# Causal attention and a channel mixer on one core: the values product in 64x64 tiles, the first queries loaded as they lie, and 16-bit copies that GpSimd may take

## The chip, the cores and the metric

The kernel runs on one core of a Trainium2 chip. TensorE (PE) multiplies, VectorE (DVE), ScalarE (ACT) and GpSimd (POOL) do the rest, SyncE (SP) issues most transfers. The metric is the device time of one execution in microseconds, as the median of several runs.

## The reference

```python
scores = scale * q @ k.T            # q, k, v: 4 batches x 12 heads x 448 x 64, float32
scores = where(upper triangle, -1e9, scores)
attn = exp(scores - max) / (sum + 1e-9)
x = attn @ v                        # heads side by side: 4 x 448 x 768
h = relu(x.T @ w_tok1) @ w_tok2     # 448 -> 256 -> 448, over tokens
u = x + h.T
out = u + relu(u @ w_ch1) @ w_ch2   # 768 -> 1536 -> 768, over channels
```

The six mixer products and the weights are handled as sums of a rounded part and its remainder, three products for one; attention runs in float32, in which PE executes each product as two instructions.

## The kernel before

Two heads of one batch form a pair, 24 pairs in all. For each pair `load_pair` loads k, q and v, `prep` turns k and q so that the 64 channels lie along partitions, `heads` makes scores, exponentials and sums, `by_tensor` (pairs 0 to 9, transposes on PE) or `by_dma` (pairs 10 to 23, a DMA transpose of 16-bit halves: a `split` before it, a `merge` behind it) turns the probabilities into the tile `pt`, and `values` multiplies them with v and copies the sums from PSUM into `u`. Every third pair is followed by `xturn` and `tokens`, each batch by `split_u`; the channel products of batches that are done (`product` and its callers) fill PE between the pairs and are alone on it from about 300 us on.

No engine's order is written out. `plan.job` records each step with its engine and costs, and `Plan.emit` hands out the steps: on a free engine the one of lowest rank whose needs are met. The rank is a number from the table PLACES, and where a step may run on more than one engine the table CHOICE says which (a, d, p, s for ACT, DVE, POOL, SP). The order is fixed when the program is built; each engine works through its list and waits at semaphores. Where the plan finds PE without work before 75 us, it puts in a product whose result is not used (`keep_warm`, L865).

PE takes its array as one 128x128 tile, two tiles of 128x64, two of 64x128 or four of 64x64. A values product before is eight (pairs 0 to 9) or four pieces per head in 128x64 tiles (L1245), then eight products for the keys and queries that are left, the tips, in 64x64 tiles (L1254). Scores (L1021) are in 64x64, transposes of probabilities and of x (L1115, L1291) in 64x128, channel and token products (L1433, L1350, L1383) in 128x128, and the first pairs' k and q are turned by 112x64 tiles (L916).

A transfer reports to one of eight semaphores (DMAHW0 to DMAHW7), which the program gives out in turn over all queues. The issue of the ninth transfer therefore waits until the first has landed, and so on.

Of the kernel before, what the change touches and what calls it, by code (L numbers as in the profile page):

```python
# [21 lines left out]
    "load_pair.blocks": {-2: (0, 1), 10: (129, 153), 12: (193, 224), 14: (242, 259), 16: (338, 293), 18: (405, 420),  # L22
        20: (522, 537), 22: (578, 591), 24: (670, 694), 26: (742, 758), 28: (831, 851), 30: (911, 927), 32: (996,
        1006), 34: (1056, 1070), 36: (1141, 1151), 38: (1205, 1220), 40: (1280, 1293), 42: (1333, 1348), 44: (1406,
        1426)},
    "load_pair.load": {0.5: (2,), 2.5: (3,), 4.5: (178,), 6.5: (209,), 8.5: (274,), 10.5: (312,), 12.5: (393,),
        14.5: (453,), 16.5: (490,), 18.5: (558,), 20.5: (615,), 22.5: (704,), 24.5: (773,), 26.5: (822,), 28.5:
        (902,), 30.5: (949,), 32.5: (1047,), 34.5: (1114,), 36.5: (1194,), 38.5: (1241,), 40.5: (1376,), 42.5:
        (1441,), 44.5: (1489,), 46.5: (1531,)},
    "load_pair.upper": {-0.2: (12,), 1.8: (15,), 3.8: (213,), 5.8: (245,), 7.8: (317,), 9.8: (380,), 11.8: (441,),  # L30
        13.8: (505,), 15.8: (519,), 17.8: (592,), 19.8: (651,), 21.8: (727,), 23.8: (821,), 25.8: (859,), 27.8:
        (938,), 29.8: (982,), 31.8: (1077,), 33.8: (1136,), 35.8: (1226,), 37.8: (1269,), 39.8: (1401,), 41.8:
        (1462,), 43.8: (1517,), 45.8: (1561,)},
    "narrow.load": {3.5: (6, 9, 16, 62, 86, 121, 114, 144), 12: (288,), 13: (371,), 14: (445,), 15: (503,), 16:
        (606,), 17: (665,), 18: (755,), 19: (818,), 20: (897,), 21: (974,), 22: (1041,), 23: (1120,), 24: (1191,),
        25: (1254,), 26: (1328,), 27: (1400,), 28: (1463,), 29: (1511,), 30: (1553,), 31: (1599,), 32: (1627,), 33:
        (1660,), 34: (1687,), 35: (1730,)},
    "narrow.size": {3.5: (32, 52, 61, 116, 133, 177, 180, 235), 12: (352,), 13: (413,), 14: (484,), 15: (545,), 16:
        (642,), 17: (705,), 18: (786,), 19: (854,), 20: (932,), 21: (1013,), 22: (1072,), 23: (1153,), 24: (1223,),
        25: (1291,), 26: (1360,), 27: (1437,), 28: (1497,), 29: (1532,), 30: (1584,), 31: (1616,), 32: (1646,), 33:  # L40
        (1676,), 34: (1712,), 35: (1748,)},
    "narrow.shift": {3.5: (37, 56, 73, 125, 142, 183, 186, 263), 12: (359,), 13: (424,), 14: (491,), 15: (554,), 16:
        (646,), 17: (710,), 18: (793,), 19: (863,), 20: (939,), 21: (1019,), 22: (1084,), 23: (1157,), 24: (1227,),
        25: (1295,), 26: (1371,), 27: (1446,), 28: (1503,), 29: (1538,), 30: (1588,), 31: (1621,), 32: (1649,), 33:
        (1678,), 34: (1720,), 35: (1750,)},
# [6 lines left out]
    "prep.turn": {-1.5: (5, 8), 10.5: (199, 216), 12.5: (253, 271), 14.5: (286, 304), 16.5: (375, 384), 18.5: (449,
        486), 20.5: (562, 577), 22.5: (609, 626), 24.5: (702, 734), 26.5: (767, 790), 28.5: (877, 895), 30.5: (943,
        995), 32.5: (1014, 1034), 34.5: (1087, 1140), 36.5: (1166, 1176), 38.5: (1229, 1239), 40.5: (1304, 1315),
        42.5: (1368, 1378), 44.5: (1440, 1456)},
    "heads.<lambda>": {0: (11, 13), 2: (51, 57), 4: (94, 101), 6: (141, 160), 8: (197, 233), 10: (251, 267), 12:
# [1921 lines left out]
```

## Time and profile before

| | |
|---|---|
| time, median of 3 runs | 537.71 us (537.52 to 538.35) |
| the profiled execution's own time | 538.04 us |
| its span in the profile | 536.2 us |
| PE busy | 529.8 us |
| DVE, ACT, POOL busy | 426.4, 314.0, 164.2 us |
| granted TensorE clock | 1.0 in the mean |

Busy time is the time in which at least one instruction of the engine runs. A row of the timeline has the start, the time from the first start to the last end, the engine, the line, the operation, the tile written and those read, shape and count; in brackets stands how long the engine had been idle and what ended that. In rows of PE the tile shape stands ahead of the moving data's, as in 64*64 64x448.

### The profile page before, as it was taken

The numbers are of one execution on the slowest core, as the hardware profiler recorded it, in microseconds if no ns is written. First come the engines' busy times: TensorE is split into PE (matmuls) and PEld (weight loads), VectorE is DVE, ScalarE is ACT, GpSimd is POOL, SyncE is SP. The second block draws the span as 40 slices with busy tenths as digits, with TensorE's granted clock in tenths as the row PEclk, the third lists the DMA queues.
The fourth block names the chain that finished last, engine by engine and source line by source line (L and its number), as shares of the span: only waits on it lengthen the run. The fifth ranks groups of instructions, "written<-read, shape, count | busy, mean of one in ns | idle before, by whom it ended". The sixth has DMA issues, their size and how long they took to land.

```text
span 536.2 us, 12037 instructions
## 1 busy us (share of the span) xinstructions
PE 529.8 (99%) x4391; PEld 460.6 (86%) x4391; DVE 426.4 (80%) x1030; ACT 314.0 (59%) x768; POOL 164.2 (31%) x220
## 2 busy tenths in 40 slices
PE   8999999999999999999999999999999999999997
PEld 4778888888888888888898899999999999999996
DVE  5998899989797999888896679677877848485665
ACT  4998898899888787789784561243232313131300
POOL 2565745444252232332452132140010012321200
PEclk9999999999999999999999999999999999999999
DMA  9966677979999998999969327648213030212147
GB/s 194 198 116 144 152 214 160 215 153 233 207 178 200 225 190 193 205 196 229 210 163 198 115 92 205 131 119 162 88 32 116 7 91 23 87 32 88 31 75 131
DMA packets 221546, 77.72 MB, mean 145 GB/s; under 512 B 195760, under 2 KB 210992, under 8 KB 221488
## 3 DMA queue, kind: packets, MB, share of 16 engines
q1 hardware_dynamic: 207984, 74.90, 63.1%
q10 hardware_dynamic: 13504, 2.07, 2.1%
q8 instruction: 34, 0.56, 0.5%
q14 instruction: 24, 0.20, 0.2%
HBM read 49.15 MB, written 14.94 MB: 120 GB/s over the span
## 4 chain that ended last, share of the span: by engine, by line
PE 94%; SPq 2%; DVE 2%; ACT 1%; DMA 1%; issue 0%; POOL 0%; DVEq 0%; POOLq 0%
PE ps L1433 33%; PE ps L1860 16%; PE ps L1765 12%; PE ps L1021 6%; PE ps L1245 6%; PE ps L1383 6%; PE ps L1350 6%; PE ps L1836 3%; PE ps L1254 1%; PE ps L1115 1%; PE ps L1291 1%; SPq L940 1%; PE ps L865 1%; ACT prob L1055 1%; DMA gh<-in_k_dram 1%; PE ps L910 0%
## 5 line engine op out<-in xcount | busy, mean ns | idle before, releaser
L1500 DVE TENSOR_TENSOR u<-ps,u 128x448 f32<-128x448 f32 x118 | 72.5, 619 | 34.2 <-PE ps L1860 28.0
L1055 ACT ACTIVATE prob<-prob,stat 128x192 f32<-128x192 f32 (+6 forms) x168 | 83.7, 501 | 14.4 <-DVE stat L1043 14.1
L643 POOL TENSOR_TENSOR wl<-wf,wh 128x768 fp32r<-128x768 f32 x26 | 49.5, 1904 | 94.4 <-ACT wh L632 59.4
L1043 DVE CUSTOM_DVE_ANT_0 prob<-ps,mask 128x128 f32<-128x128 f32 (+6 forms) x168 | 63.3, 415 | 7.3 <-PE ps L1021 6.9
L634 POOL TENSOR_SCALAR prob<-prob,stat 128x64 f32<-128x64 f32 (+6 forms) x80 | 43.8, 559 | 55.4 <-DVE stat L1077 42.9
L1433 PE MATMUL ps<-uh,wh 128*128 128x448 f32 x144 | 53.7, 373 | 0.0
L1433 PE MATMUL ps<-gh,wh 128*128 128x448 f32 x144 | 52.9, 367 | 0.0
L1433 PE MATMUL ps<-gh,wl 128*128 128x448 f32 x144 | 52.7, 366 | 0.0
L1433 PE MATMUL ps<-gl,wh 128*128 128x448 f32 x144 | 52.7, 366 | 0.0
L1433 PE MATMUL ps<-uh,wl 128*128 128x448 f32 x144 | 52.7, 366 | 0.0
L1433 PE MATMUL ps<-ul,wh 128*128 128x448 f32 x144 | 52.7, 366 | 0.0
L632 ACT ACTIVATE wh<-wf 128x768 fp32r<-128x768 f32 x27 | 22.5, 846 | 51.2 <-PE ps L1860 25.8
L1021 PE MATMUL ps<-kq,kq 64*64 64x64 f32 (+5 forms) x768 | 45.4, 356 | 0.0
L1021 PEld LDWEIGHTS ps<-kq,kq 64*64 64x64 f32 x768 | 26.6, 133 | 15.5 <-issue 9.6
L1245 PE MATMUL ps<-pt,vraw 128*64 128x128 f32 (+2 forms) x544 | 37.3, 284 | 0.0
L1245 PEld LDWEIGHTS ps<-pt,vraw 128*64 128x64 f32 x544 | 28.2, 137 | 9.8 <-issue 2.1
L1795 DVE TENSOR_TENSOR kq<-kq,ps 128x448 f32<-128x448 f32 x35 | 21.2, 619 | 14.8 <-PE ps L1765 14.2
L1055 ACT ACTIVATION_READ_ACCUMULATOR prob<-prob,stat 128x1 f32 x168 | 32.1, 191 | 0.0
L638 ACT COPY pt<-pt 128x384 uint16<-128x384 uint16 (+3 forms) x41 | 31.6, 830 | 0.8 <-DMA pt<-prob 0.8
L1860 PE MATMUL ps<-u,wh 128*128 128x448 f32 (+1 forms) x110 | 31.0, 363 | 0.0
L1433 PEld LDWEIGHTS ps<-uh,wh 128*128 128x128 f32 x144 | 27.0, 188 | 2.8 <-issue 0.2
L1433 PEld LDWEIGHTS ps<-gl,wh 128*128 128x128 f32 x144 | 27.1, 188 | 2.5 <-DVE gl L1468 0.2
(222 smaller groups left out, 1403.2 us busy)
## 6 DMA issues: line engine op xcount, KB each, us to landing
wraw<-in_moe_w_ch_dram SPq DMA_DIRECT2D x24, 768.0 KB, 5.4
wf<-scratch SPq DMA_DIRECT2D x30, 384.0 KB, 3.1
scratch<-wf SPq DMA_DIRECT2D x24, 384.0 KB, 4.8
vraw<-in_v_dram SPq DMA_DIRECT2D x44, 96.0 KB, 3.4
kq<-in_k_dram SPq DMA_DIRECT2D x60, 56.0 KB, 3.7
kq<-in_q_dram SPq DMA_DIRECT2D x56, 56.0 KB, 2.4
out_dram<-h1l SPq DMA_DIRECT2D x24, 56.0 KB, 2.7
out_dram<-h1h SPq DMA_DIRECT2D x24, 56.0 KB, 2.2
```

What stands on the lines that cost most here:

```text
L634: eng[e].tensor_scalar(dst, src, scale, 0.0, op0=ALU.mult, op1=ALU.add)
L643: eng[e].tensor_tensor(dst, a, b, op=ALU.subtract)
L1021: nc.tensor.matmul(scores[n].tile[lanes, to:at], lhsT=qe.tile[LANES[j], c * QC:(c + 1) * QC], rhs=ke.tile[LANES[j], slice(*keys)], start=T ...
L1043: nc.vector.tensor_tensor_reduce(out=part(c, r), in0=ps.tile[:, at:at + wide(c)], in1=mask[:, S - QC:S + P] if c == 2 else mask[:, S - wid ...
L1055: nc.scalar.activation(part(c, r), part(c, r), AF.Exp, bias=stat.tile[:, 0, AT[c]:AT[c] + 1], scale=-1.0, accum_out=stat.tile[:, 1, AT[c]: ...
L1245: nc.tensor.matmul(to, lhsT=s.tile[:, kb, j], rhs=rhs, start=(n in first_of), stop=False)
L1350: nc.tensor.matmul(ps.tile[:, :PART], lhsT=w[:, c, m * P:(m + 1) * P], rhs=x.tile[:, c, :], start=(n == 0), stop=(n == len(work) - 1),)
L1383: nc.tensor.matmul(ps.tile[:, :S], lhsT=h.tile[:, m, o * P:(o + 1) * P], rhs=w[:, m, :], start=(n == 0), stop=(n == 3 * NM - 1),)
L1433: nc.tensor.matmul(ps.tile[:, :S], lhsT=x.tile[:, at_:at_ + P], rhs=y, start=(n == 0 and i == 0), stop=(n + 1 == w[2] and i == 2),)
L1500: eng[e].tensor_tensor(u, ps.tile[:, :S], u, op=ALU.add)
L1765: nc.tensor.matmul(ps.tile[:, :S], lhsT=l()[:, t * P:(t + 1) * P], rhs=r, start=(t == 0 and n == 0), stop=(t == half - 1 and n == 2),)
L1860: nc.tensor.matmul(ps.tile[:, cols], lhsT=l.tile[:, t * P:(t + 1) * P], rhs=r.tile[:, cols], start=(n == 0), stop=(n == 3 * len(fs) - 1),)
```

## The change

It has four parts.

1. `values` cuts each 128-row product into two 64-row ones. Rows 0 to 63 add up in one PSUM bank and rows 64 to 127 in another, so that scores, values and tips all use 64x64 tiles; the tips become part of the second step. The sum of the two banks is new: a copy of one bank to `u` (ACT or DVE), then an addition of the other on DVE over 384 columns.
2. q of pair 0 is loaded by rows in one transfer on ACT's queue and turned by PE; before it came in four transfers and DVE turned it.
3. `split` and `merge` of the 16-bit halves may run on GpSimd.
4. PLACES and CHOICE are new throughout, one line of each is shown.

```diff
-    "xturn.twice": {1: "p", 5: "p", 9: "a", 13: "p", 17: "p", 21: "p", 25: "p", 29: "a", 33: "p", 37: "a", 41: "p",
+    "xturn.twice": {1: "p", 5: "a", 9: "a", 13: "a", 17: "p", 21: "a", 25: "p", 29: "p", 33: "p", 37: "a", 41: "a",
...
@@ words
-            nc.vector.tensor_copy(out, in_)
+            eng[e].tensor_copy(out, in_)
@@ load_rows
-            {"sp": 535.0 if g < ONCE else 1070.0}, load, holds=[home, s], rank=2.0 * g + RL,
+            {"sp" if g else "act": 535.0 if g < ONCE else 1070.0}, load, holds=[home, s], rank=2.0 * g + RL,
@@ load_pair, and prep likewise
+    def lies(g, nm):
+        return nm != "v" and g < WHOLE and (g, nm) != (0, "k")
-            if 0 < g < WHOLE and nm != "v":
+            if lies(g, nm):
@@ by_dma
-                {"act": act_sb(2 * nb * P), "dve": dve2(2 * nb * P)}, split, parts, [probs[r], both], rank, lock=True
+                {"act": act_sb(2 * nb * P), "dve": dve2(2 * nb * P), "pool": 195.0 + 1.0 * 2 * nb * P}, split, parts, [probs[r], both], rank, lock=True
@@ merged
+            costs["pool"] = 195.0 * n + 1.15 * 2 * nb * P
@@ values
-        def chunks(n, j):
+        def chunks(n, j, half):
...
-                rhs = pt.tile[:, 1 - j if c in OVER else j, o:o + stride * (nq - 1) + 1:stride]
+                rhs = pt.tile[LANES[half], 1 - j if c in OVER else j, o:o + stride * (nq - 1) + 1:stride]
...
                 for n in part:
-                    for j in range(2):
-                        kb, to, rhs = chunks(n, j)
-                        nc.tensor.matmul(to, lhsT=s.tile[:, kb, j], rhs=rhs, start=(n in first_of), stop=False)
+                    for half in range(2):
+                        for j in range(2):
+                            kb, to, rhs = chunks(n, j, half)
+                            nc.tensor.matmul(to, lhsT=s.tile[LANES[half], kb, j], rhs=rhs, start=n == 0, stop=False)
+                for half, kb, o, c in ENDS if part[0] else ():
+                    for j in range(2):
+                        nc.tensor.matmul(
+                            banks[half].tile[LANES[j], c * QC:(c + 1) * QC],
+                            lhsT=(ends if half else s).tile[LANES[half], kb, j], rhs=tip(o, c, j, half),
+                            start=False, stop=(o == 9),
+                        )
...
-        def tips(e):
...
-        def evac(e):
+        def nought(e):
             if t == 0:
                 make(u, [P, NT, S], F32)
-            copy(e, u.tile[:, t, 3 * QC:], ps.tile[:, 3 * QC:S])
-            copy(e, u.tile[:, t, :3 * QC], low.tile[:, :3 * QC])
+            copy(e, u.tile[:, t], low.tile[:, :S])
+
+        def evac(e):
+            nc.vector.tensor_tensor(u.tile[:, t, QC:], ps.tile[:, QC:S], u.tile[:, t, QC:], op=ALU.add)
```

The order moves in three places that matter here. The first is the head of the transfers. On SP these are the first issues before: k of pair 0 in four, v, q of pair 1 (ul), k of pair 1 (uh).

```order
L940 DMA kq_96<-in_k_dram 32x14x32 x4
L949 DMA vraw_89<-in_v_dram 128x3x64 [waits DMAHW1_49]
L949 DMA vraw_89<-in_v_dram 128x3x64 [waits DMAHW3_49]
L953 DMA vraw_89<-in_v_dram 64x2x64 [waits DMAHW5_49]
L892 DMA ul_118<-in_q_dram 112x8x64 [waits DMAHW6_49]
L686 DMA wh_124<-in_moe_w_tok_dram 128x512 [waits DMAHW7_49]
L892 DMA uh_128<-in_k_dram 112x8x64 [waits DMAHW0_49]
```

Now q of pair 0, v of pair 0 and k of pair 6 come first on ACT. Its load of q is the first transfer of the program and so the first that reports to DMAHW0.

```order
L891 DMA ul_96<-in_q_dram 112x8x64
L951 DMA vraw_89<-in_v_dram 128x3x64 x2
L955 DMA vraw_89<-in_v_dram 64x2x64
L942 DMA gh_113<-in_k_dram 32x14x32
L942 DMA gh_113<-in_k_dram 32x14x32 [waits DMAHW1_49]
```

and on SP (k of pair 0, then k and q of pair 1 and k of pair 2 by rows):

```order
L942 DMA kq_98<-in_k_dram 32x14x32 x3
L942 DMA kq_98<-in_k_dram 32x14x32 [waits DMAHW0_49]
L891 DMA uh_111<-in_k_dram 112x8x64 [waits DMAHW2_49]
L891 DMA ul_96<-in_q_dram 112x8x64 [waits DMAHW4_49]
L891 DMA uh_111<-in_k_dram 112x8x64 [waits DMAHW6_49]
```

Moved: v has gone to ACT, k of pair 6 has come to the front, the fourth part of pair 0's k stands behind a wait for q's landing, and the weights stand behind four row loads.

The second place is the head of PE and DVE. On PE, before the first scores (L1021), stand 16 products of L865 before; now 6, the turn of q (L915), 5 more (L864), then the scores (L1023). This is DVE's head now, with kq_98 the loaded k, ps_119 the turned q, and L1045 the first reductions of scores:

```order
L990 STREAM_TRANSPOSE kq_129<-kq_98 128x448 [waits DMAHW2_49,DMAHW6_49,DMAHW1_49,DMAHW0_49]
L633 TENSOR_SCALAR kq_136<-ps_119 128x448 [waits PE_49]
L1045 ISA prob_0_85,stat_163<-ps_143,mask 128x448 [waits PE_49,Pool_49]
L1045 ISA stat_163 128x1
L1045 ISA prob_0_85,stat_163<-ps_144,mask 128x64 [waits PE_49]
```

Before, its two first rows were two transposes (L988), of k and of q. Now q's copy out of PSUM stands behind k's transpose.

The third place is a values product on PE, here of pair 10, with pt the probabilities and vraw and vend the values; before:

```order
L1433 MATMUL ps_2136<-gh_2092,wl_2010 128x448
L1245 MATMUL ps_2157<-pt_2065,vraw_89 64x256 x2
L1245 MATMUL ps_2158<-pt_2065,vraw_89 64x128 x2
L1245 MATMUL ps_2157<-pt_2065,vraw_89 64x256 x2
L1245 MATMUL ps_2157<-pt_2065,vraw_89 64x128 x2
L1021 MATMUL ps_2178<-kq_1883,kq_1919 64x448 x2
```

and now:

```order
L1434 MATMUL ps_2284<-gh_2206,wl_2157 128x448
L1249 MATMUL ps_2303<-pt_2159,vraw_89 64x256 x2
L1249 MATMUL ps_2304<-pt_2159,vraw_89 64x256 x2
L1249 MATMUL ps_2303<-pt_2159,vraw_89 64x128 x2
L1249 MATMUL ps_2304<-pt_2159,vraw_89 64x128 x2
...
L1252 MATMUL ps_2303<-pt_2159,vraw_89 64x64 x2
L1252 MATMUL ps_2304<-pt_2159,vend_90 64x64 x2
L1023 MATMUL ps_2337<-kq_2108,kq_2154 64x448 x2
```

Each piece stands twice, once for each half of the rows, with the same columns as before; from the first piece to the scores behind the tips the tile shape stays the same.

## Rows read from the trace of the kernel before

**Rows 1.** The page, busy us (share of the span) and instructions.

```profile
PE 529.8 (99%) x4391; PEld 460.6 (86%) x4391; DVE 426.4 (80%) x1030; ACT 314.0 (59%) x768; POOL 164.2 (31%) x220
```

**Rows 2.** Waits of PE: engine, line, for whom; us in total, times, longest.

```profile
PE ps L916 <- DMA uh<-in_k_dram: 0.7, 1, 0.7
PE ps L1115 <- DVE stat L1043: 0.4, 1, 0.4
```

**Rows 3.** Timeline of PE from its start.

```profile
1.49 5.15 PE L865 MATMUL ps<-mask 128*128 128x512 bf16 x16 [1.49 <-POOL mask L650]
6.57 1.79 PE L1021 MATMUL ps<-kq,kq 64*64 64x448 f32 x32
...
9.36 0.82 PE L865 MATMUL ps<-mask 128*128 128x512 bf16 x3
...
12.37 0.61 PE L865 MATMUL ps<-mask 128*128 128x512 bf16 x2
12.90 1.79 PE L1021 MATMUL ps<-kq,kq 64*64 64x448 f32 x32
```

**Rows 4.** Timeline of all engines, 0 to 14 us: the first issues, the first transposes.

```profile
0.72 1.95 SPq L940 DMA_DIRECT2D kq<-in_k_dram  x4
...
2.82 1.05 SPq L949 DMA_DIRECT2D vraw<-in_v_dram  x2
...
4.94 1.17 DVE L988 STREAM_TRANSPOSE kq<-kq 128x448 f32<-128x448 f32 x2 [4.94 <-DMA kq<-in_k_dram]
```

**Rows 5.** Line 940, 0 to 6 us: from issue to landing.

```profile
DMA to landing us min/median/max: 2.1/2.5/2.9
```

**Rows 6.** DMA issues, 0 to 14 us: count, KB each, median us to landing.

```profile
ul<-in_q_dram SPq DMA_DIRECT2D x2, 224.0 KB, 4.3
```

**Rows 7.** Timeline of DVE: the first and the last score reduction of pair 0.

```profile
7.70 0.62 DVE L1043 CUSTOM_DVE_ANT_0 prob<-ps,mask 128x448 f32<-128x448 f32 x1 [0.77 <-PE ps L1021]
...
10.12 0.08 DVE L1043 DVE_READ_ACCUMULATOR2_ANT stat<- 128x1 f32 x1
```

**Rows 8.** Timeline of PE: pair 21's values product, its tips, and the scores behind.

```profile
264.29 1.52 PE L1245 MATMUL ps<-pt,vraw 128*64 128x256 f32 x16
265.74 0.27 PE L1254 MATMUL ps<-pt,vraw 64*64 64x64 f32 x2
...
266.02 1.74 PE L1021 MATMUL ps<-kq,kq 64*64 64x448 f32 x32
```

**Rows 9.** Timeline of PE: half a pair's scores ahead of tips.

```profile
137.56 0.99 PE L1021 MATMUL ps<-kq,kq 64*64 64x448 f32 x12
138.36 0.22 PE L1254 MATMUL ps<-pt,vraw 64*64 64x64 f32 x1
```

**Rows 10.** Timeline of PE: the same scores between token products.

```profile
163.64 0.28 PE L1350 MATMUL ps<-xl,w1hi 128*128 128x256 f32 x1
163.85 0.99 PE L1021 MATMUL ps<-kq,kq 64*64 64x448 f32 x12
164.77 0.39 PE L1350 MATMUL ps<-xh,w1hi 128*128 128x256 f32 x1
164.99 0.28 PE L1350 MATMUL ps<-xl,w1hi 128*128 128x256 f32 x1
165.11 0.28 PE L1350 MATMUL ps<-xh,w1lo 128*128 128x256 f32 x1
```

**Rows 11.** The page, groups: busy us, mean ns of one, then idle before.

```profile
L1500 DVE TENSOR_TENSOR u<-ps,u 128x448 f32<-128x448 f32 x118 | 72.5, 619 | 34.2 <-PE ps L1860 28.0
L643 POOL TENSOR_TENSOR wl<-wf,wh 128x768 fp32r<-128x768 f32 x26 | 49.5, 1904 | 94.4 <-ACT wh L632 59.4
```

**Rows 12.** Groups of DVE by line, shapes together.

```profile
L640 DVE COPY pt<-pt 128x512 uint16<-128x512 uint16 (+3 forms) x43 | 23.7, 597 | 3.2 <-DMA pt<-prob 3.1
L640 DVE COPY prob<-prob 128x1024 uint16<-128x1024 uint16 (+1 forms) x26 | 16.8, 664 | 1.4 <-ACT prob L632 0.7 <-POOL prob L634 0.4
```

**Rows 13.** Groups of POOL by line and shape.

```profile
L634 POOL TENSOR_SCALAR wh<-wf 128x768 fp32r<-128x768 f32 x15 | 12.7, 848 | 50.0 <-DVE wf L699 34.4 <-PE ps L1021 7.2 <-PE ps L1433 6.1
```

More of the change, by code (lines that the diff above doesn't have):

```diff
@@ L21 @@
 PLACES = {
[L22 to L45, printed above, removed]
@@ L52 @@
[L52 to L56, printed above, removed]
[3 rows of a table removed]
@@ new lines @@
+    "values.evac": {0: (141,), 2: (182,), 4: (276,), 6: (314,), 8: (374,), 10: (424,), 12: (505,), 14: (575,), 16:
+        (628,), 18: (670,), 20: (721,), 22: (811,), 24: (884,), 26: (968,), 28: (1026,), 30: (1112,), 32: (1199,),
+        34: (1237,), 36: (1325,), 38: (1388,), 40: (1484,), 42: (1546,), 44: (1596,), 46: (1649,)},
+    "xturn.turn": {1: (211,), 5: (321,), 9: (461,), 13: (582,), 17: (674,), 21: (817,), 25: (979,), 29: (1122,), 33:
+        (1260,), 37: (1397,), 41: (1573,), 45: (1653,)},
@@ new lines @@
+    "channels.down": {28.5: (699,), 28.75: (685,), 29: (747,), 29.25: (720,), 29.5: (800,), 29.75: (761,), 36:
[6 rows of a table added]
+    "add.plus": {-6: (708, 711, 762, 732, 821, 826, 1117, 1126, 1068, 1084, 1188, 1150, 1146, 1156, 1209, 1261,
[6 rows of a table added]
+    "store.turn": {-5: (1741, 1756, 1770, 1780, 1788, 1798, 1843, 1854, 1862, 1872, 1879, 1892, 2235, 2236, 2243,
+        2244, 2249, 2250, 2254, 2259, 2263, 2267)},
+    "store.send": {-5: (1743, 1760, 1773, 1783, 1790, 1800, 1848, 1858, 1866, 1873, 1883, 1894, 2237, 2240, 2245,
+        2248, 2255, 2253, 2258, 2260, 2266, 2268)},
@@ new lines @@
+    "reread.load": {-4.95: (1834, 1846), -4.94: (1853, 1863, 1904, 1906), -4.93: (1921, 1936, 1976, 1977), -4.92:
+        (1994, 1999, 2035, 2036), -4.91: (2060, 2062, 2104, 2105), -4.9: (2128, 2133, 2170, 2171, 2183, 2202)},
+    "group.up": {54: (1855,), 54.18: (1860,), 54.36: (1864,), 54.54: (1867,), 54.72: (1871,), 54.9: (1876,), 74.25:
+        (2191,), 74.43: (2204,), 74.61: (2208,), 74.79: (2199,), 74.97: (2212,), 75.15: (2217,)},
+    "hidden.relu": {-6: (1869, 1882, 1916, 1943, 1945, 1947, 1996, 2006, 2015, 2016, 2065, 2076, 2085, 2078, 2130,
+        2145, 2147, 2150, 2207, 2211, 2227, 2219, 2214, 2223)},
@@ new lines @@
+    "combined.sum_.do": {-4.94: (1881, 1885, 1890, 1893), -4.93: (1954, 1957, 1961, 1967), -4.92: (2014, 2017, 2022,
+        2025), -4.91: (2084, 2086, 2090, 2094), -4.9: (2151, 2153, 2157, 2161)},
+    "group.product.do": {55.44: (1884,), 55.71: (1889,), 55.98: (1907,), 56.25: (1929,), 56.52: (1902,), 56.79:
[5 rows of a table added]
+    "group.first.do": {-6: (1891, 1952, 2019, 2095, 2160)},
+    "group.plus.do": {-6: (1909, 1914, 1935, 1938, 1941, 1940, 1942, 1993, 1995, 1998, 2002, 2004, 2013, 2011, 2061,
+        2064, 2068, 2070, 2072, 2082, 2075, 2127, 2129, 2138, 2141, 2143, 2144, 2146, 2201, 2205, 2203, 2206, 2209,
+        2226, 2213)},
@@ L243 @@
+    "spared.hi": {-4.9: (2177, 2215)},
+    "spared.lo": {-4.9: (2178, 2220)},
+    "finish.plus": {-6: (2270, 2271, 2273, 2281)},
+    "finish.turn": {-6: (2272, 2274, 2280, 2283)},
+    "finish.evac": {-6: (2275, 2277, 2282, 2285)},
+    "finish.send": {-6: (2278, 2279, 2284, 2286)},
 }
 CHOICE = {
[6 rows of a table removed]
-    "token_weights.<lambda>": {3.5: "papppppp"},
-    "token_weights.rest_of": {3.5: "ppppdpdp"},
-    "heads.guard": {0: "pp", 2: "dp", 4: "pd", 6: "ap", 8: "pp", 10: "pp", 12: "pa", 14: "pa", 16: "da", 18: "dp",
-        20: "pp", 22: "pp", 24: "pp", 26: "ap", 28: "pp", 30: "da", 32: "ad", 34: "dp", 36: "aa", 38: "aa", 40:
-        "ap", 42: "pp", 44: "dd", 46: "da"},
@@ L1216, in values @@
         flat_ = g < TURN
-        def chunks(n, j):
+        def chunks(n, j, half):
             if flat_:
-                which, kb, c, step, nq, o, stride = PIECES[n]
-                out = banks[which].tile[LANES[j]].rearrange("p (c q) -> p c q", q=QC)[:, c:c + step * (nq - 1) + 1:step]
-                rhs = pt.tile[:, 1 - j if c in OVER else j, o:o + stride * (nq - 1) + 1:stride]
+                _, kb, c, step, nq, o, stride = PIECES[n]
+                out = banks[half].tile[LANES[j]].rearrange("p (c q) -> p c q", q=QC)[:, c:c + step * (nq - 1) + 1:step]
+                rhs = pt.tile[LANES[half], 1 - j if c in OVER else j, o:o + stride * (nq - 1) + 1:stride]
                 return kb, out, rhs
@@ L1226, in chunks @@
             view = pt.tile.rearrange("p o (j q) -> p o j q", j=2)
-            return kb, banks[c == 1].tile[LANES[j], c * QC:(c + nq) * QC], view[:, o, 1 - j if c in MIXED else j]
+            out = banks[half].tile[LANES[j], c * QC:(c + nq) * QC]
+            return kb, out, view[LANES[half], o, 1 - j if c in MIXED else j]
         def tip(o, c, j, half):
@@ L1249, in values @@
             )
-        def tips(e):
-            for half, kb, o, c in ENDS:
-                for j in range(2):
-                    nc.tensor.matmul(
-                        banks[half].tile[LANES[j], c * QC:(c + 1) * QC],
-                        lhsT=(ends if half else s).tile[LANES[half], kb, j], rhs=tip(o, c, j, half),
-                        start=False, stop=(o == 9),
-                    )
-        prev = plan.job({"pe": 282.0}, tips, [prev], [ps, low, s, ends, pt, u], rank, tiled=2)
```

257 lines of the change are left out of this document (125 added, 132 removed), and 210 rows, old and new, of tables (CHOICE, PLACES).

## The prediction

> **What bounds the kernel now.** I read the page first. PE is busy for 529.8 of the span's 536.2 us [rows 1]; no other engine comes near. The waits of PE are next: behind the start there are hardly two, 0.7 us for a load and 0.4 us for a reduction, both before 50 us [rows 2]. So this kernel's time is a plain sum: the moment of the first scores, the PE work behind it, the few waits. An engine that gets slower or faster elsewhere changes nothing until PE waits for it. The timeline of PE shows the start: 16 unused products from 1.49 us, the first scores at 6.57 us, the second pair's at 12.90 us [rows 3]. All sums go against the profiled execution, 538.04 us with a span of 536.2; the median of the runs is 0.33 us lower, and the forecast at the end is put on the median.
>
> **Part 1, the product in 64x64 tiles.** It looks as if half-size tiles, four at once, should be quicker. They are not: each 128x64 tile streamed 768 columns per pair; cut in two, each half streams the same 768, only beside the other. What can be saved is the change of tile shape between L1245 and the tips, one per pair, and what can be lost is the cost of twice as many instructions.
>
> The price of a change: token products start 0.12 us apart (164.99 to 165.11); ahead of scores the step is 0.21, behind them 0.22, so 0.09 and 0.10 are lost there [rows 10]. The same half of scores takes 0.80 us up to the tips, of its own shape but for its entry, and 0.92 between token products [rows 9, 10], another 0.12. Together 0.31 for two changes, 0.155 each. Pair 21's product takes 1.45 and its tips 0.28 us, 1.73 in all [rows 8]; without the change at its entry and the one at the tips, two at about 0.1 to 0.15, that leaves 1.45 to 1.53 of streaming. For the new form the nearest row is that of the scores behind it, which also stream 896 columns through each of four tiles (768 and the tips' 128): L1021, 1.74 us from first start to last end [rows 8], which holds the last instruction's tail. I take the streaming as unchanged, 0. The ends: four tiles overlap no better than scores do, +0.04 us per pair, or better by as much; over 24 pairs plus or minus 1.0 us.
>
> Counted in PE's order, 24 changes inside products go. But the new list sets the transposes and products more finely between channel products, and almost as many come back: 132 changes before, 128 after, and behind the first scores 131 and 125. Six fewer at 0.155 are 0.93 us. Against it, entries into 128x128, which cost 0.10 at the entry alone where entry into 64x64 costs about half of that, rise from 40 to 53; 13 times 0.05 gives back 0.6. I take **-0.3 us**, between -0.9 and 0.
>
> The sum of two banks gives DVE 24 additions of 384 columns; an addition of 448 takes 0.619 [rows 11], so 0.53 each, 12.7 us. The same list takes 11 splits at 0.66 and 11 merges at 0.60 off DVE [rows 12], 13.9 us, so that DVE's load stays as it is. For PE that is 0, as long as no product waits for a bank; its cover is that PE hardly waits for DVE today [rows 2]. The Trainium skill, TensorEngine Tiling (Array Packing), section PSUM Bottleneck, says against this part that tiling speeds up TensorE but not the evacuation of PSUM, which may become the bottleneck. By the row the sum gets 0 from it; by the rule DVE would be the bound, which is rival E.
>
> **Part 2, the start.** This is the largest term. Before, SP issues the four parts of k without a wait, in 1.95 us from 0.72 on; the ninth transfer of the program, v, is issued at 2.82, when the first k has landed (0.72 and the least landing time of 2.1) [rows 4, 5]: the wait for a semaphore's former owner is real. Both transposes start at 4.94 and take 1.17 us, and the scores follow at 6.57, 0.46 us behind [rows 3, 4]. Now k's fourth part is the ninth transfer, and it waits for the load of q, 224 KB in one piece, issued at about 0.7 us. Such a load lands after 4.3 us in a crowd [rows 6]; 56 KB take 2.1 to 2.9 [rows 5]. At the head of its queue, with k's three parts beside it, I put it at 3.5 us, so at 4.2. The fourth part is then issued, lands 2.5 us later, at 6.7, is turned by DVE (half of 1.17), and only then does DVE copy the turned q, which I price like the other half. With the same 0.1 to 0.4 behind, scores start at about 8.05 instead of 6.57: **+1.45 us** (q landing between 2.9 and 4.3 us after its issue: +0.8 to +2.4). PE's turn of q falls in the time before, where unused products stood, and costs nothing.
>
> What is late next: the second pair's scores. From first scores to last reduction takes 10.20 - 6.57 = 3.6 us [rows 3, 7]; then on DVE come a guard of 0.2, k's copy of 0.6 and 0.25 to the start, 4.7 in all. PE's scores take 1.8, and three turns stand behind them, each like the one that now fills PE from 8.36 to 9.36 [rows 3], 1.0 at most; so PE is free at 4.5 to 4.8, waits 0.2 or nothing, and those scores start at 12.75, as early as today. That doesn't give the start back: up to there the new PE list holds no unused product behind the first scores, the old one five, and the others come later.
>
> **Unused products.** 27 stand in both lists, but 16 before the first scores and 11 behind, and now 11 and 16. Two take 0.61 us and three 0.82 [rows 3], 0.21 each. Five more in the part that counts: **+1.05 us**.
>
> **Waits.** Of the two rows [rows 2] nothing need stay, as both operands are loaded and reduced in another order; I put one at 0.2 us at the second scores and 0.6 elsewhere, against 1.1: **-0.3 us** (-1.1 to +2).
>
> **Part 3, GpSimd's copies.** It takes 16 splits and 22 merges; the trace has none of that kind. A copy of 1,024 elements goes by the nearest rows: one input, 768 elements, 0.848 [rows 13], so 1.13; two inputs, 1.904 [rows 11], so 2.54; a gain would ask for less than DVE's 0.66 [rows 12], which neither row gives. I take 1.13, as a copy has one input. POOL is busy for 164.2 us of 536 [rows 1], and 38 copies at about 1 us make it 200: hidden, 0, unless merges come so late that a product waits (rival C).
>
> **The sum.** +1.45 - 0.3 + 0 + 1.05 - 0.3 = +1.9 us, 539.9 for the profiled execution, **539.6** for the median. Its own range, with the ends above, is 538.2 to 541.5.
>
> **Rivals.** Rival B, not slower: k's fourth part isn't held. If q's load lands within 2.2 us, as SP would come to that part no sooner, k is there by 4.9 as today, DVE works the same 1.17 us, and the first term goes: 539.9 - 1.45 = 538.4, 538.1 for the median. For it speaks that 56 KB land in 2.1 [rows 5] on a queue just as empty; against it that q is four times as large.
>
> Rival C, slower: GpSimd's copies at the upper end, 2.54 us. Each of the 14 later pairs has about three of them in its chain; 1.4 us more each, with a reserve that I guess at two of the three, leaves some 0.3 to 0.5 us of waiting per pair: +4 to +7, about 545. Against it: these copies have one input.
>
> Rival D: the change does less than it says. The four tiles of a product do not overlap and run like two pairs in turn: then a product takes 1.3 us more, 24 times, +31. The scores, four tiles at once, speak against it [rows 8].
>
> Rival E, by DVE: the additions of 12.7 us lie in the first 300 us while the copies taken off fall elsewhere in the pair, and a product's banks come free late by 0.2 us per pair: +5, 544.5.
>
> Rival F, faster: the three small terms lie at their lower ends, product -1.0, changes -0.6 and waits -0.8 below my values; that makes 537.2 with the start as I price it, and 535.8 with rival B.
>
> **How the numbers follow.** Chances: the forecast 0.55, B 0.15, C 0.09, D 0.01, E 0.08, F 0.12. About 0.2%, 1.1 us, is what a measurement tells here: slower begins at 538.8, faster ends at 536.6. The forecast's case is slower in 0.47 and same in 0.08; B is same in 0.11, faster in 0.04; C, D and E are slower, 0.18; F is same in 0.05, faster in 0.07. Sums: faster 0.11, same 0.24, slower 0.65. The range leaves out the better half of F and the worse half of C and E: 536.9 to 543.5.
>
> **What would show it.** The first scores at 7.3 to 9.0 us, with SP's fourth k issued more than 1 us behind its third; the second pair's scores near 12.8. A product with its tips, from its first start to the scores behind, at 1.5 to 1.65 us. In the sum of PE's changes no gain above 1 us. POOL's copies of 1,024 at 1.0 to 1.4. PE's waits below 2 us in all, none for pt. I am wrong if the scores start by 7 us, if a product takes under 1.45, or if a wait of PE on DVE or POOL stands high in its list.

## The result, and the profile after

The changed kernel took 543.67 us (median of 4 runs, 542.54 to 546.67), the kernel before beside it 538.03: a ratio of 1.0123, 95% interval 1.0104 to 1.0141. Slower was forecast, at 539.6; the excess is 5.6 us where 1.9 were expected. The profiled execution is the fastest of the four, 542.54 us with a span of 540.8, which is 4.5 us above the one of before.

The page's first part. It answers to [rows 1]: PE's busy time grew by 2.7 us and the span by 4.6, so PE also stood idle 1.9 us longer. GpSimd got 26 us, ScalarE lost 6.5.

```profile
PE 532.5 (98%) x4951; PEld 462.3 (85%) x4951; DVE 427.9 (79%) x1029; ACT 307.5 (57%) x740; POOL 190.0 (35%) x249
```

PE's waits: engine, tile and line, for whom; us in total, times, longest. They answer to [rows 2]. The first row stands before the first product in both kernels. New are waits for VectorE (DVE) by channel products (L1434), each a single one.

```profile
PE ps L864 <- POOL mask L649: 1.5, 1, 1.5
PE ps L1023 <- DVE kq L633: 0.9, 1, 0.9
PE ps L1434 <- DVE stat L1045: 0.8, 1, 0.8
PE ps L1434 <- DVE u L1501: 0.5, 1, 0.5
```

PE's timeline from the start, to lay beside [rows 3]: eleven unused products around the turn of q (L915), the first scores at 8.20 instead of 6.57 us, the second pair's at 12.72.

```profile
1.49 2.74 PE L864 MATMUL ps<-mask 128*128 128x512 bf16 x6 [1.49 <-POOL mask L649]
4.42 1.67 PE L915 MATMUL ps<-ident,ul 112*64 112x112 f32 x16 [0.19 <-DMA ul<-in_q_dram]
6.03 1.25 PE L864 MATMUL ps<-mask 128*128 128x512 bf16 x5
8.20 1.79 PE L1023 MATMUL ps<-kq,kq 64*64 64x448 f32 x32 [0.93 <-DVE kq L633]
...
12.72 1.53 PE L1023 MATMUL ps<-kq,kq 64*64 64x448 f32 x22
```

What leads there, against [rows 4]: SP's four issues for k now take 3.89 us, as the fourth waits for q, and VectorE's transpose waits for that part until 6.99 us (two timelines, SP and DVE).

```profile
0.72 3.89 SPq L942 DMA_DIRECT2D kq<-in_k_dram  x4
```

```profile
6.99 0.65 DVE L990 STREAM_TRANSPOSE kq<-kq 128x448 f32<-128x448 f32 x1 [6.99 <-DMA kq<-in_k_dram]
7.56 0.59 DVE L633 TENSOR_SCALAR kq<-ps 128x448 f32<-128x448 f32 x1
```

A product in PE's timeline, for [rows 8]: 1.53 us from its first start to the scores behind (124.15 to 125.68), where pair 21 took 1.73 before. This one stands behind scores, of its own tile shape; pair 21 stands behind channel products. Behind those the new product takes 1.58 us (108.17 to 109.76, and three more), so like against like 0.15 us are saved.

```profile
124.15 1.49 PE L1249 MATMUL ps<-pt,vraw 64*64 64x256 f32 x32
125.45 0.22 PE L1252 MATMUL ps<-pt,vraw 64*64 64x64 f32 x1
...
125.68 0.99 PE L1023 MATMUL ps<-kq,kq 64*64 64x256 f32 x20
```

GpSimd's copies (groups by line and shape; the mean in ns stands behind the busy time): splits of 1,024 elements took 1.12 us, merges of as many 1.44. The lower of the two bounds from [rows 11, 13], 1.13, holds for the splits.

```profile
L639 POOL COPY prob<-prob 128x1024 uint16<-128x1024 uint16 x5 | 5.6, 1118 | 4.2 <-ACT prob L631 2.9 <-issue 1.2
L639 POOL COPY pt<-pt 128x1024 uint16<-128x1024 uint16 x3 | 4.3, 1435 | 6.2 <-PE ps L1434 4.4 <-DMA pt<-prob 1.8
```

**Where the 4.6 us of span stand.** For behind 9 us I fitted one price per streamed column for each kind of product, and one for each change of tile shape, to PE's start-to-start times in all profiles with the same kinds of work; what a block takes beyond is called a stall. Before and after: first scores +1.6; unused products behind them 1.98 and 2.88 (+0.9); changes 23.7 and 22.9 (-0.8); other work +0.4; stalls 2.1 and 3.6 (+1.5); and from the last 1,017 channel products on, whose median step was 204 instead of 203 ns, +0.8; 0.2 are left over. Of the stalls, 3.0 us lie at 100 to 170 us, where before had none.

Where they begin: VectorE's timeline, then PE's. VectorE stands 3.31 us for a block of k, is behind in its queue, and PE waits at 111.15 for the addition (L1501) that is to free a bank.

```profile
107.50 0.65 DVE L990 STREAM_TRANSPOSE kq<-kq 128x448 f32<-128x448 f32 x1 [3.31 <-DMA kq<-in_k_dram]
...
110.42 1.12 DVE L1501 TENSOR_TENSOR u<-ps,u 128x448 f32<-128x448 f32 x2
```

```profile
111.15 0.45 PE L1434 MATMUL ps<-gh,wh 128*128 128x448 f32 x1 [0.46 <-DVE u L1501]
```

This is 0.5 of the 3.0 us. The longest wait there is PE's for VectorE's reductions of scores (L1045). VectorE's rows have no pause from 122.41 us up to it, behind a wait of 0.50 us for k, so they don't tell by themselves whether late loads or a full queue made it late.

```profile
127.49 0.47 PE L1434 MATMUL ps<-gh,wh 128*128 128x448 f32 x1 [0.82 <-DVE stat L1045]
```

### The profile page after: what moved, and what is told of

It is laid out like the page before. It is cut to its first block, busy times and chain, and to the rows that moved or that the text cites. A ratio compares the mean times of both kernels' runs of the same rounds, so it can differ in the third digit from the quotient of the medians.

```text
span 540.8 us, 13141 instructions
## 1 busy us (share of the span) xinstructions
PE 532.5 (98%) x4951; PEld 462.3 (85%) x4951; DVE 427.9 (79%) x1029; ACT 307.5 (57%) x740; POOL 190.0 (35%) x249
## 4 chain that ended last, share of the span: by engine, by line
PE 87%; DMA 5%; ACT 2%; DVE 2%; SPq 1%; issue 1%; POOL 0%; DVEq 0%; ACTq 0%; POOLq 0%
PE ps L1434 29%; PE ps L1861 16%; PE ps L1766 12%; PE ps L1023 6%; PE ps L1249 5%; PE ps L1351 5%; PE ps L1384 4%; PE ps L1837 3%; PE ps L1117 2%; DMA wraw<-in_moe_w_ch_dram 2%; DMA kq<-in_k_dram 2%; PE ps L1292 1%; DMA pt<-prob 1%; PE ps L1252 1%; PE ps L864 1%
## 5 line engine op out<-in xcount | busy, mean ns | idle before, releaser
L1501 DVE TENSOR_TENSOR u<-ps,u 128x448 f32<-128x448 f32 x118 | 72.6, 620 | 39.2 <-PE ps L1861 35.2
L1057 ACT ACTIVATE prob<-prob,stat 128x256 f32<-128x256 f32 (+6 forms) x168 | 83.9, 502 | 12.2 <-DVE stat L1045 11.3
L642 POOL TENSOR_TENSOR wl<-wf,wh 128x768 fp32r<-128x768 f32 x23 | 44.0, 1915 | 99.9 <-ACT wh L631 97.0
L631 ACT ACTIVATE wh<-wf 128x768 fp32r<-128x768 f32 x30 | 24.9, 842 | 76.3 <-PE ps L1861 46.7
L1045 DVE CUSTOM_DVE_ANT_0 prob<-ps,mask 128x64 f32<-128x64 f32 (+6 forms) x168 | 64.1, 413 | 4.8 <-PE ps L1023 4.3
L633 POOL TENSOR_SCALAR prob<-prob,stat 128x384 f32<-128x384 f32 (+6 forms) x90 | 47.7, 542 | 45.4 <-DVE stat L1079 38.3
L1434 PE MATMUL ps<-gh,wh 128*128 128x448 f32 x144 | 53.6, 372 | 1.3 <-DVE stat L1045 0.8
L1434 PE MATMUL ps<-uh,wh 128*128 128x448 f32 x144 | 54.1, 376 | 0.0
L1434 PE MATMUL ps<-gh,wl 128*128 128x448 f32 x144 | 52.8, 367 | 0.0
L1434 PE MATMUL ps<-uh,wl 128*128 128x448 f32 x144 | 52.8, 367 | 0.0
L1434 PE MATMUL ps<-gl,wh 128*128 128x448 f32 x144 | 52.7, 366 | 0.0
L1434 PE MATMUL ps<-ul,wh 128*128 128x448 f32 x144 | 52.6, 366 | 0.0
L1023 PE MATMUL ps<-kq,kq 64*64 64x64 f32 (+5 forms) x768 | 46.7, 359 | 0.9 <-DVE kq L633 0.9
L1023 PEld LDWEIGHTS ps<-kq,kq 64*64 64x64 f32 x768 | 26.8, 133 | 19.3 <-issue 9.4
L1249 PE MATMUL ps<-pt,vraw 64*64 64x128 f32 (+2 forms) x1088 | 38.1, 279 | 0.1
L1249 PEld LDWEIGHTS ps<-pt,vraw 64*64 64x64 f32 x1088 | 31.5, 133 | 6.7 <-issue 2.2
L990 DVE STREAM_TRANSPOSE kq<-kq 128x448 f32<-128x448 f32 x29 | 18.6, 641 | 18.3 <-DMA kq<-in_k_dram 15.2
L1434 PEld LDWEIGHTS ps<-gh,wh 128*128 128x128 f32 x144 | 27.0, 188 | 4.4 <-DVE stat L1045 1.1
L1434 PEld LDWEIGHTS ps<-uh,wh 128*128 128x128 f32 x144 | 27.1, 188 | 3.2 <-issue 0.3
L1434 PEld LDWEIGHTS ps<-gh,wl 128*128 128x128 f32 x144 | 27.0, 188 | 2.8 <-POOL wl L642 0.4
```

What stands on the lines that cost most here:

```text
L631: nc.scalar.activation(dst, src, AF.Copy, scale=scale)
L633: eng[e].tensor_scalar(dst, src, scale, 0.0, op0=ALU.mult, op1=ALU.add)
L642: eng[e].tensor_tensor(dst, a, b, op=ALU.subtract)
L1023: nc.tensor.matmul(scores[n].tile[lanes, to:at], lhsT=qe.tile[LANES[j], c * QC:(c + 1) * QC], rhs=ke.tile[LANES[j], slice(*keys)], start=T ...
L1045: nc.vector.tensor_tensor_reduce(out=part(c, r), in0=ps.tile[:, at:at + wide(c)], in1=mask[:, S - QC:S + P] if c == 2 else mask[:, S - wid ...
L1057: nc.scalar.activation(part(c, r), part(c, r), AF.Exp, bias=stat.tile[:, 0, AT[c]:AT[c] + 1], scale=-1.0, accum_out=stat.tile[:, 1, AT[c]: ...
```

## The experiments

In each of them the order of all other instructions on every engine is kept as it was, by letting the planner see the old costs and exchanging only what is issued. Times are medians; ratios are to the kernel before, which ran beside.

**The changed kernel again.**

> The changed kernel once more, unaltered. In its first comparison the profiled execution was 4.5 us above the one of before, the median of the runs 5.6. Theory W (the excess over the forecast is waits of PE for a late VectorE, between 58 and 161 us, 1.5 to 2 us in the profiled execution and more where loads land later): again 4.5 to 5.6 us above before, with a wider spread of its runs than that of before. Rival N (one disturbed comparison): 3.5 us or less above.

543.76 us, ratio 1.0106 (1.0086 to 1.0127), runs from 541.9 to 545.5; those of before spread over 2.1. Profile: stalls of 2.6 us at 100 to 170 us. The excess is real, and theory W's place for it too.

**The start undone.**

```
+if g == 0:                     # in the load of rows
+    s.tile = flat(home.tile[:, 0])[:, :S]
+    for n in range(4):
+        j, o = divmod(n, 2)
+        eng[e].dma_start(
...
+for _ in range(0 if g else 5): # in the turn on PE
+    keep_warm(e)
...
+if g == 0:                     # in the copy on VectorE
+    nc.vector.transpose(make(x, [P, S], F32), s.tile)
+    return
```

> Changed kernel with one part undone: the queries of pair 0 come in four block loads and are transposed on VectorE, five unused products stand where PE turned them. All other instructions keep their order on every engine. By the forecast's first step the scores start near 6.6 us and the end comes 1.4 to 1.6 us earlier than in the changed kernel. Rival: the late VectorE gives the time back in waits further on, then 0 to 0.7 us earlier only.

548.22 us, ratio 1.0191 (1.0173 to 1.0209): 4.5 us slower than the changed kernel, which neither side expected. The first scores came at 7.00, the second pair's at 15.39. ScalarE's queue shows why: fourteen transfers instead of eleven stand at its head, the later ones held until an earlier one has landed, so that it comes to its first own work, the load of the exponential's table, at 11.54 us (8.11 in the changed kernel). The second pair's copy of k on VectorE stands behind the first pair's sums of exponentials, for which VectorE waited 3.92 us, and PE waited 3.78 us for the copy. Behind that wait the granted clock of PE was 0.50 (16 to 18 us), its lower level, 1.2 GHz, and the second pair's scores took 3.00 us instead of the first pair's 1.79, so the 4.5 us are in part the clock's. ScalarE's queue, then PE's scores:

```profile
4.80 3.13 ACTq L956 DMA_DIRECT2D gh<-in_k_dram  x4
9.42 1.34 ACTq L965 DMA_DIRECT2D vraw<-in_v_dram  x2
10.90 0.61 ACTq L969 DMA_DIRECT2D vraw<-in_v_dram  x1
11.54 1.28 ACT L1071 ACT_TABLE_LOAD   x1 [11.54 <-DMA gh<-in_k_dram]
```

```profile
15.39 3.00 PE L1037 MATMUL ps<-kq,kq 64*64 64x448 f32 x32 [3.78 <-DVE stat L1093]
```

So it was tried again with ScalarE's four block loads (of k, pair 5) on SP, behind SP's second weight load.

```
+if pick.key == ("load_pair.blocks", 10.0, 0):
+    late = pick.fn
+else:
+    pick.fn(e)
+if pick.key == ("narrow.load", 3.5, 1):
+    late("sp")
```

> Changed kernel with the start undone as before, and the four block loads that ScalarE issued behind it given to SP, so that ScalarE reaches its first exponential no later than in the changed kernel. By the forecast's first step the first scores come at 7.0 us instead of 8.1 and the end 1 to 1.5 us earlier. Rival: the pairs behind the first are held by ScalarE and VectorE anyway, unused products and waits fill the time that is won, and the end comes within 0.5 us of the changed kernel.

543.05 us, ratio 1.0097 (1.0073 to 1.0121); first scores at 6.71. Of 1.3 us at the start at most 0.7 reached the end, and that is not told apart from nothing. PE's waits show where it went: the turns of later row loads.

```profile
PE ps L932 <- DMA uh<-in_k_dram: 1.1, 1, 1.1
PE ps L926 <- DMA uh<-in_k_dram: 1.0, 1, 1.0
```

**No unused products behind the first scores.**

```
-self.filler.fn(e)
+if now < 8000.0:
+    self.filler.fn(e)
```

> Changed kernel without the 16 unused products behind the first scores, nothing else moved. By the forecast's term (0.21 us each, all on the path) 3.4 us earlier. Rival: they stand where PE would wait for its operands anyway; then the waits grow by most of it and the end comes 0 to 1 us earlier. A third outcome: the granted clock falls in the gaps and the kernel gets slower.

542.79 us, ratio 1.0098 (1.0078 to 1.0118), 1.0 us below the changed kernel of the same group, with intervals that overlap. The stalls grew to 7.8 us from 4.8. The rival holds: these products mostly stand where PE would wait.

**The old product in the new list.**

```
...
-nc.tensor.matmul(to, lhsT=s.tile[LANES[half], kb, j], rhs=rhs, start=n == 0, stop=False)
+nc.tensor.matmul(to, lhsT=s.tile[:, kb, j], rhs=rhs, start=(n in first_of), stop=False)
...
-copy(e, u.tile[:, t], low.tile[:, :S])        # and the addition behind it
+copy(e, u.tile[:, t, 3 * QC:], ps.tile[:, 3 * QC:S])
+copy(e, u.tile[:, t, :3 * QC], low.tile[:, :3 * QC])
```

> Changed kernel with the values product of before (128x64 tiles, tips behind it in 64x64, both copies of the result by the engine that copied one bank, no addition on VectorE), everything else in its place. By the forecast's price (24 changes of tile shape at 0.1 to 0.155 us) 2.4 to 3.7 us slower. Rival E (the 24 additions on VectorE make it late): the waits of 1.7 us go with them, so slower by 0.7 to 2 us only.

545.83 us, ratio 1.0148 (1.0130 to 1.0166), 2.1 us slower. By the fit the changes cost 29.6 us instead of 22.9 (165 of them instead of 128), and the stalls at 100 to 170 us were gone. The 6.7 us are the fit's price, 0.18 us, for 37 changes. Of them 2.1 reach the end (3.0 between the two profiled spans); the stalls of 3.0 us take most of the rest, and what takes the remainder isn't shown. The outcome fits rival E by size, so the additions had to be separated from PE's pace.

**The old product, with work of the additions' length on VectorE.**

```
...                            # the old product, as above
+nc.vector.tensor_tensor(x[:, 3 * QC:], ps.tile[:, 3 * QC:S], x[:, 3 * QC:], op=ALU.max)
+nc.vector.tensor_tensor(x[:, 3 * QC:5 * QC], ps.tile[:, 3 * QC:5 * QC], x[:, 3 * QC:5 * QC], op=ALU.max)
```

> Changed kernel with the values product of before, as in the run that undid it alone, but VectorE still gets work of the additions' length in their place: two instructions of 256 and 128 columns that take the maximum of a bank and of its copy, 24 times. Theory E: the stalls at 100 to 170 us come back, 1.5 to 3 us slower than with the old product alone (545.8 us there). Rival L, or any theory by which the pace of PE alone makes it wait: within 0.7 us of that run.

545.07 us, ratio 1.0138 (1.0116 to 1.0160): no slower than without that work. PE's windows (busy us of the stretch, then granted clock, DMA share, GB/s), first of the changed kernel, then of this one: 1.52 us idle, and none.

```profile
100.00:175.00 75.00, 73.48 (x739) 1.00 0.94 192
```

```profile
100.00:175.00 75.00, 75.00 (x669) 1.00 0.94 192
```

Theory E falls as the cause of these stalls by itself: VectorE carries the work without PE noticing, as long as PE is slower.

**The new product without the additions.**

```
-nc.vector.tensor_tensor(u.tile[:, t, QC:], ps.tile[:, QC:S], u.tile[:, t, QC:], op=ALU.add)
```

> Changed kernel without the 24 additions of the two banks on VectorE (13.1 us by their mean of 548 ns); each values product then lacks the half of the keys that lies in the other bank. Everything else in its place. Theory E (VectorE's in-order work, made longer by the additions, is what PE waits for): the stalls of PE at 100 to 170 us (2.6 to 3.0 us in the two profiles of the changed kernel) go, 2 to 4 us faster than the changed kernel, 540 to 541.5 us. Rival L (PE has become faster than the loads): the stalls stay, within 1 us of the changed kernel.

541.91 us, ratio 1.0068 (1.0049 to 1.0086): 1.9 us below the changed kernel (543.76, measured in another group; the intervals of the two ratios touch at 1.0086), but stalls of 2.0 us stayed at 100 to 170 us. Neither theory alone: the additions cost up to 2 us once PE is at their heels; the stalls there do not hang on them.

**One exchange in SP's queue.**

```
+if pick.key[:2] == ("load_pair.load", 22.5):
+    late = pick.fn, e
+else:
+    pick.fn(e)
+if pick.key == ("load_pair.blocks", 24, 1):
+    late[0](late[1])
```

> Changed kernel with one swap in SP's queue: the load of pair 11's values stands behind the loads of pair 12's keys and queries instead of ahead of them (seven transfers exchanged, nothing else moved). In the changed kernel VectorE stood 3.3 us at 107.5 us for these keys, and PE waited at 108 to 115 us behind it. Theory L (late loads make VectorE late and PE wait): that wait of VectorE shrinks to about 1 us, the stalls of PE at 108 to 115 us (0.8 to 1.6 us) go, and the end comes 0.5 to 1.5 us earlier. Rival Q (VectorE's own load makes it late): stalls and time stay within 0.5 us.

546.21 us, ratio 1.0132 (1.0107 to 1.0156): not faster. VectorE's wait for keys shrank as theory L had it, but another took its place: VectorE's waits at 90 to 172 us, then ScalarE's timeline.

```profile
DVE xl L648 <- ACT xh L637: 4.3, 2, 3.5
DVE pt L645 <- DMA pt<-prob: 2.0, 2, 1.6
DVE kq L996 <- DMA kq<-in_k_dram: 1.7, 3, 0.6
```

```profile
112.30 0.83 ACT L643 COPY prob<-prob 128x768 uint16<-128x768 uint16 x1 [4.32 <-POOL prob L639]
```

The later values were waited for by GpSimd, it by ScalarE, and that by VectorE and PE. This run shows that the queues are coupled, not which of them is to blame.

**GpSimd's copies undone, and done alone in the kernel before.**

```
-pick.fn(e)
+to = INSTEAD.get(pick.key[0], {}).get(pick.key[1], {}).get(pick.key[2])
+pick.fn({"a": "act", "d": "dve", "p": "pool"}[to] if to else e)
```

> Changed kernel with the 29 splits and merges of GpSimd (16 and 13) done by the engine that did them in the kernel before, 14 on ScalarE and 15 on VectorE, in their place in the order. Rival C (GpSimd's copies come late or hold VectorE through a port that both use): 1 to 2 us faster, and the stalls of PE between 120 and 165 us go. Theory W (VectorE has no reserve there): VectorE gets some 10 us of work more, 0 to 3 us slower.

546.49 us, ratio 1.0149 (1.0116 to 1.0181), above the changed kernel in each of its three comparisons, though the interval overlaps those of two of them (1.0104 to 1.0141 and 1.0086 to 1.0127): no sign of rival C, the copies rather relieve VectorE and ScalarE.

> Kernel before with 29 splits and merges on GpSimd alone (those that the changed kernel gives it), everything else in its place. By the forecast's third part (hidden) within 0.5 us of before. Rival C: slower by 1 to 4 us, with waits of PE or VectorE on GpSimd.

539.69 us, ratio 1.0017 (1.0006 to 1.0029): by the ratio 0.9 us slower. In the old list they are not quite hidden.

**The product alone in the kernel before, and with GpSimd's copies.**

```
...                            # the product as in the change
-copy(e, u.tile[:, t, 3 * QC:], ps.tile[:, 3 * QC:S])
-copy(e, u.tile[:, t, :3 * QC], low.tile[:, :3 * QC])
+copy(e, u.tile[:, t], low.tile[:, :S])
+nc.vector.tensor_tensor(u.tile[:, t, QC:], ps.tile[:, QC:S], u.tile[:, t, QC:], op=ALU.add)
```

> Kernel before with the 64x64 values product alone (product and tips together, one bank copied by the engine that copied before, the other added on VectorE behind it), everything else in its place. By the forecast's price of the changes (24 at 0.1 to 0.155 us, streaming unchanged) 2.4 to 3.7 us faster. Rival E (VectorE's 24 additions, 12.7 us, make PE wait): no gain, or slower by up to 2 us, with waits of PE on VectorE in the profile.

542.18 us, ratio 1.0065 (1.0043 to 1.0087): slower. By the fit the changes fell from 23.7 to 19.6 us, by more than forecast, and the stalls rose from 2.1 to 7.5. In this list the addition stands right behind ScalarE's copy and often right ahead of the transposition of u (L1292): VectorE waits for the one and PE for the other (PE's waits, then VectorE's).

```profile
PE ps L1292 <- DVE u L1267: 2.2, 3, 1.4
...
PE ps L916 <- DMA uh<-in_k_dram: 1.3, 1, 1.3
```

```profile
DVE u L1267 <- ACT u L632: 9.0, 17, 1.7
```

> Kernel before with two of the three parts, its order kept: the 64x64 product (its addition three VectorE instructions behind the bank's copy) and the 29 splits and merges on GpSimd. The start and the list stay as before. VectorE gets 13.1 us of additions and loses 15 copies (about 9 us), PE loses 24 changes (3.7 us by the forecast's price). Theory E: PE's waits eat 1 to 3 us of the 3.7, so 535.5 to 538 us, faster than before by 0 to 2.5 us; then the refitted list and the start cost 5 us or more in the changed kernel. Rival (the additions cost PE more than the changes give): 540 us or above, as in the run with the product alone.

548.90 us, ratio 1.0200 (1.0181 to 1.0219). Worse still: three instructions further back, the addition lets PE wait 5.8 us in five places ahead of the transposition. Behind the longest of these waits, 2.9 us up to 131.94 us, the granted clock was 0.55 and 0.60 in the next two stretches of 2 us, so part of the loss is the clock's. The rival holds: in an order that was not made for it the product loses.

```profile
PE ps L1311 <- DVE u L1285: 5.8, 5, 2.9
```

**Fewer loads.**

```
 def load(e, s=s, src=src):          # values
     kept(s)
+    if g >= 8:
+        return
```

> Changed kernel that leaves out the loads of the values for pairs 8 to 23 (their products use the values of an earlier pair; 48 transfers and their issues fall out of SP's queue, nothing else moved). Theory L (loads and the in-order queue that issues them set the pace of the first 170 us, and a PE that is freed of tile changes waits for them): VectorE's waits for keys at 90 to 172 us (4.4 to 6.1 us in two profiles) fall below 2 us, the stalls of PE at 100 to 170 us (2.6 to 3.0 us) below 1 us, 1.5 to 3 us faster. Rival Q (the engines' own work sets it): stalls stay, within 1 us.

> The changed kernel unaltered, beside the three others of this group. 4.5 to 6 us above before, its runs spread over 2 to 4 us; its profile shows between 100 and 170 us stalls of PE of 2 to 3 us in all, at places that move by some us from profile to profile (theory L: landings of loads decide them).

In one group: 540.50 us, ratio 1.0040 (1.0027 to 1.0053), against 542.91, ratio 1.0085 (1.0067 to 1.0103) of the changed kernel. The stalls at 100 to 170 us are gone (-0.2 and 3.0 us), VectorE's waits for k there too. By the medians 2.4 us of the excess go, and 2.7 us above the kernel before stay. The window of PE of the first, and the largest wait of VectorE at 90 to 172 us, first without these loads, then with them:

```profile
100.00:175.00 75.00, 75.00 (x754) 1.00 0.89 179
```

```profile
DVE prob L1047 <- PE ps L1025: 1.1, 4, 0.4
```

```profile
DVE kq L990 <- DMA kq<-in_k_dram: 5.6, 4, 3.0
```

Theory L holds: with the same product, additions and order on the other engines, the stalls go when loads leave SP's queue. Whether it is the transfers themselves or their issue one behind the other isn't separated, and no run took the same loads out of the kernel before.

**The product only where nothing is late.** `fine = g % 2 == 0`, `g >= 10 and g % 2 == 0` and `g >= 14 and g % 2 == 0` choose the new form in the kernel before.

> Kernel before with the 64x64 product for the 12 even pairs alone, those behind which no transposition of the result stands; odd pairs keep the old product. Forecast's price: 12 changes at 0.155, 1.9 us less. With the product in all pairs PE waited 3.1 us for VectorE's additions, nearly all at those transpositions, and some more for loads in the first 160 us. If the additions at the transpositions were the loss, this gives 1 to 2 us less than before (536 to 537). If a faster PE meets late loads all the same, 0 to 1.5 us more than before.

540.73 us, ratio 1.0047 (1.0032 to 1.0062). By the ratio that is 2.5 us more than before, beyond both of the expectations. The transpositions of u were not all of the loss.

> Kernel before with the 64x64 product for the even pairs from 10 on alone (seven products, 109 us and later). 7 changes at 0.155 less, 1.1 us. Theory L (PE meets late loads up to 170 us only): 0.5 to 1.1 us faster than before, faster than both kernels. Rival: no gain, since every queue is fitted to the old length of a product.

537.19 us, ratio 0.9990 (0.9975 to 1.0006).

> The kernel before with the 64x64 product for the even pairs from 10 on, once more: its first comparison gave 0.7 us less than before, with an interval that holds zero. Theory L: 0.4 to 1.1 us less again. If the gain was chance, within 0.3 us of before.

537.34 us, ratio 0.9994 (0.9983 to 1.0005). Both times a little less, not told from nothing.

> Kernel before with the 64x64 product for the even pairs from 14 on alone (five products, 166 us and later, where no stall of PE was seen). 5 changes at 0.155: 0.8 us less than before. If PE meets late loads there too, no gain.

536.98 us, ratio 0.9977 (0.9964 to 0.9989): 1.1 us faster, where 0.8 was expected for five changes. It is the one version that beats both kernels clear of noise, in one comparison.

## Why the forecast came out wrong

**The step that failed is "Waits", -0.3 us.** It measured +1.5 in the profiled execution, still inside the ends given for it (-1.1 to +2), and by the same fit +2.7 and +4.1 in the two later ones, outside of them. The sentence that carried it was that an engine which changes speed elsewhere "changes nothing until PE waits for it", with the two short waits of [rows 2] read as a reserve. They show that PE did not wait; not by how little. PE was the slowest by so small a margin that taking tile changes from it let the others come up: old product no stall at 100 to 170 us, new product 2.6 to 3.0, old product with the additions' work none, new product with fewer loads none. One of the forecast's own signs of being wrong came true: waits of PE for VectorE stand high in its list (0.9, 0.8 and 0.5 us).

**The product.** Its streaming (0) was right, and 1.53 to 1.58 us per product lies within the range given. The -0.3 for changes came out at -0.8. What it hid is that two large amounts cancel: the new list would have 165 changes with the old product, 5.9 us more by the fit than the kernel before, and the old one 108 with the new.

**The start.** On the changed kernel's side it was right: q landed and the fourth k was issued as worked out, the scores came at 8.20 for 8.05, the second pair's at 12.72 for 12.75. The reading of the kernel before was not. VectorE's transposes end at 6.11 us there [rows 4], but PE has no pause ahead of the scores at 6.57 [rows 3]: the 16 unused products run right up to them, and how long these take varies. In the run with five new products, whose start is that of before, they take 6.38 us instead of 5.15, and the scores come at 7.80:

```profile
1.49 6.38 PE L865 MATMUL ps<-mask 128*128 128x512 bf16 x16 [1.49 <-POOL mask L650]
```

In the eight profiles with the old start the first scores come at 6.57 to 7.92 us (median 7.1), in the ten with the new start at 7.55 to 8.20 (median 7.8). The old start's earliest happened to stand beside the new one's latest, so the +1.6 is in part luck and about 0.8 is nearer to what the start costs in place; won back, it gave 0.7 us at most at the end.

**Unused products.** +0.9 for +1.05 in place, but taking 16 of them away gave at most 1.0 us, not 3.4. They are a sign of waiting, not its cause.

**GpSimd's copies.** Their price was right for the splits (1.12 us for 1.13) and low for the merges (1.44); "hidden" was right for the changed kernel, and no run shows rival C in it. **Rival E** had the right direction and nearly the size (544.5), but in the changed kernel the additions explain at most 2 us and not the stalls at 100 to 170 us; in the old list it is seen in plain rows.

The profiled execution came out 2.6 us above its forecast of 539.9: 1.8 for waits, 0.8 for the end from the last channel products on and 0.4 for other work, less 0.5 for changes. Of the 0.8 its two repeats show 0.2, so most of it is no property of the change (below). The median lies 1.1 us above the profiled execution, where the forecast put it 0.3 below; the stalls, 3.6, 4.8 and 6.2 us in three profiles, change from run to run. Theories W and L fit together: the run with fewer loads shows that the stalls at 100 to 170 us hang on loads. The chain from a load to each single stall isn't shown, and of the excess that stays without these loads no single run tells the parts.

## What to carry to other kernels

A busy share of 99% tells who is slowest, not by how much; before work is taken off that engine, look in each stage at how long the others stand ready, above all for loads that land just when they are used. A sum of terms by place is no sum of what each is worth: take one away alone before believing it. And put a faster form where the engines that feed it have slack, here the last five of twelve candidates, for 0.2%.

## What the runs showed of the hardware

- The last 1,017 channel products, the same in each run of the changed kernel, took 207.8 us from start to start in its first profile and 206.8 in its two repeats. The run with the old product repeats the first profile within 0.1 ns in the mean of every stretch of 80 steps, and the two repeats so repeat each other (205.8 and 202.6 ns in the sixth stretch). What decides between the two isn't known.
- Transfers issued on a compute engine's queue hold its arithmetic: three more on ScalarE moved its first own work from 8.11 us to 11.54.
- PE's granted clock fell behind long waits: 0.50 at 16 to 18 us behind a wait of 3.78 us, and 0.55 at 132 to 134 us behind one of 2.88. Behind the first of these waits 32 score instructions took 3.00 us, nearly all at the lower level, 1.2 GHz; the same 32 took 1.79 at the higher one, 2.4.
- A change of tile shape inside a product costs about as the rows of before said: 0.15 us by the products behind channel products (1.73 and 1.58 us), 0.18 by the fit over all profiles.
